# A Fourier-mixing layer and an ELU MLP on one core: DRAM reads of Z and Bs by writing unit, w_out in 4 KB runs, the bias spread by a matmul

## The chip, the core and the metric

The kernel runs on one core of a Trainium2 chip. A core has five engines with queues of their own: TensorE (PE, with its weight loads shown as PEld), VectorE (DVE), ScalarE (ACT), GpSimd (POOL) and SyncE (SP, which here only issues transfers). The metric is the device time of one launch in microseconds; less is better.

## The reference

The input x has 8 sequences of 3008 positions and 256 channels, in float32. Each sequence goes through a real Fourier transform over its positions, a complex 256x256 linear map with a bias, a soft threshold at 0.01, and the inverse transform. Each position's 256 numbers then go through a two-layer network with 2048 hidden units and an ELU between.

```python
X = np.fft.rfft(x, axis=1)                       # x: (8, 3008, 256)
Yr = Xr @ w_r - Xi @ w_i + b_r
Yi = Xr @ w_i + Xi @ w_r + b_i
Yr = np.sign(Yr) * np.maximum(np.abs(Yr) - 0.01, 0.0)      # Yi likewise
y = np.fft.irfft(Yr + 1j * Yi, n=3008, axis=1)
h = y @ w_in                                     # w_in: (256, 2048)
g = np.where(h > 0, h, np.exp(np.minimum(h, 0)) - 1)
out = g @ w_out                                  # w_out: (2048, 256)
```

## The kernel before

**Transform in four matmul stages.** 3008 is 47 x 64, so the transform of a sequence is made of one over 64 points (stage A), one over 47 points (stage X), the linear map with the threshold (stage M), and back over 64 points (stage B) and 47 points (stage Y). The twiddle tables M1 to M4 are computed on the chip in the prologue: iota on POOL, range reduction on DVE, sine on ACT. Stages A, M, B and Y sum over a different index than the one that the stage before left on the partitions, and twice that takes a trip through DRAM: A's results go to a DRAM tile DA (L155, L157) and come back as Z, with 96 partitions of 32 slots (`load_Z`, L159 to L164); B's results go to DB (L260, L265) and come back as Bs, four tiles of 96 partitions and 8 slots (`load_Bs`, L267 to L272).

A sequence is 6 A units, 8 X units, 12 M groups, 6 B units and 8 Y units. X unit u reads slots 8(u//2) to 8(u//2)+8 of Z, on all 96 partitions, and Y unit u reads the one tile Bs of its slots. One A unit writes four of the 24 rows of DA, one B unit four of the 24 rows of DB; the row index lies on the partitions of what is read back, so every slot of Z needs all six A units.

**The network.** `front` (L705) makes 256 hidden units of 512 positions as four matmuls (L715), ACT takes the exponential, DVE and POOL finish the ELU (L740, L742, L752, L754), and `back` (L757) multiplies with w_out (L773), two slots later. A slot is one such half block. 47 slots make one sequence.

**Order of the work.** It is written out by hand, engine by engine, in program order. The prologue does stages A to B of sequence 0 and A of sequence 1, with dummy matmuls (`idle_pe`, L295) in PE's gaps. Then the main loop (L844) runs 376 slots; `plan` (L800) puts one unit of the next sequence's transform into most slots (`f0`, before `front`), and loads and other small work after it (`f1`). The four Bs loads of a sequence are put behind A unit 1, the two Z loads behind A unit 5.

**Queues.** SP issues the DA, Z, DB, Bs, w_in, bias and output transfers in program order and waits in place: a load that waits for a write's landing holds everything behind it. POOL issues x (L116) and w_out (L583) among its arithmetic; `gate` (L585) is a tiny POOL copy that makes POOL wait for a tile before it issues what follows.

**Bias.** `bias_bc` holds the bias on all 128 partitions; it is read from DRAM with a zero step over 128 partitions (L526 to L530) and added by DVE (L202). For half of the first sequence's M groups PE adds it instead: `bias_p` holds the bias as three bfloat16 summands in partitions 0, 32 and 64, and a matmul with ones spreads it (L189). Six small loads (L304) and DVE and ACT steps (L601, L602, L607 to L610) make `bias_p`.

**Weights of the network.** w_out comes in two transfers in runs of 1 KB, w_in in four quarters that are scaled to bfloat16 by `scale_w_in` (L655): quarters 0 and 1 on DVE, 2 on ACT, 3 on DVE in two halves in slots 3 and 4. Four POOL instructions (L520 to L523) cast w_r and w_i into `wcat_r` and `wcat_s`.

Of the kernel before, what the change touches and what calls it, by code (L numbers as in the profile page):

```python
# [8 lines left out]
ALU = mybir.AluOpType  # L9
# [10 lines left out]
N1 = 47  # L20
# [9 lines left out]
def kernel(  # L30
# [47 lines left out]
    zp = ctx.enter_context(tc.tile_pool(name="zp", bufs=1))  # L78
    wk2 = ctx.enter_context(tc.tile_pool(name="wk2", bufs=2))
    wk3 = ctx.enter_context(tc.tile_pool(name="wk3", bufs=3))  # L80
    wk4 = ctx.enter_context(tc.tile_pool(name="wk4", bufs=4))
# [47 lines left out]
    def unit_A(b, u, alone=False, on_dve=False, ahead=False):  # L129
        ci, uu = u // 2, u % 2  # L130
        if uu == 0:
            if ahead and ci > 0:
                A_of[b, ci] = late3.tile([P, 8, D], BF16, name="A", tag="gT")
            elif alone:
                A_of[b, ci] = wk4.tile([P, 8, D], BF16, name="A", tag="Bs")
            else:
                A_of[b, ci] = wk2.tile([P, 8, D], BF16, name="A", tag="A")
# [3 lines left out]
        dav = DA_of[b].rearrange("j p d -> p j d")  # L141
# [9 lines left out]
        )  # L151
        j0 = 8 * ci
# [6 lines left out]
    def load_Z(b, s0, s1):  # L159
# [3 lines left out]
        dv = DA_of[b].rearrange("j (h c s) d -> (j h c) s d", h=2, c=2)  # L163
        nc.sync.dma_start(Z_of[b][:, s0:s1, :], dv[:, s0:s1, :])  # L164
# [102 lines left out]
    def load_Bs(b, w):  # L267

        Bs = wk4.tile([4 * K1, 8, D], BF16, name="Bs", tag="Bs")
        dv = DB_of[b].rearrange("k (c h m) d -> (k c h) m d", c=2, h=2)  # L270
        nc.sync.dma_start(Bs[:], dv[:, 8 * w : 8 * w + 8, :])
        Bs_of[b, w] = Bs  # L272

    def unit_Y(b, u, alone=False, on_dve=False):
# [3 lines left out]
        yT, Bs = yT_of[b], Bs_of[b, w]  # L278
        ps = unit_ps("yps", alone)
        psv = ps[:].rearrange("p a (k j) -> p (a k) j", j=P)  # L280
        for j in range(8):
            nc.tensor.matmul(  # L282
                psv[:, j, 0 : 2 * N1], lhsT=Bs[:, j, dt * P : dt * P + P], rhs=M4[:],
# [16 lines left out]
    brow, rest = (wk3.tile([P, 2 * D], F32, name="yb", tag="yb") for _ in range(2))  # L300
    nc.vector.memset(brow[:], 0.0)
    for o, bv in ((0, b_r), (D, b_i)):
        for k in range(3):
            nc.sync.dma_start(  # L304
                brow[32 * k : 32 * k + 1, o : o + D],
                bass.AP(tensor=bv.tensor, offset=bv.offset, ap=[[0, 1], [1, D]]),
            )
    idle_pe(9)
    xts = []
# [3 lines left out]
    with tc.tile_pool(name="stagep", bufs=1) as stagep:  # L313
# [41 lines left out]
        pcol = iota("pcol", [P, 1], [[0, 1]], cm=1)  # L355
        srow = iota("srow", [P, 2 * NS], [[0, 2], [1, NS]])
# [52 lines left out]

        k4h = col(dve, qcol, 0.5, ALU.mult, -0.25, ALU.add)  # L410
# [87 lines left out]
        pool.tensor_tensor(v4[:], v4[:], r4[:], ALU.subtract)  # L498

# [17 lines left out]
        fA(5)  # L517
        nc.sync.dma_start(w_r_f[:], w_r.rearrange("(c p) e -> p c e", p=P))
        nc.sync.dma_start(w_i_f[:], w_i.rearrange("(c p) e -> p c e", p=P))
        pool.tensor_copy(wcat_r[:, :, 0:D], w_r_f[:])  # L520
        pool.tensor_copy(wcat_r[:, :, D : 2 * D], w_i_f[:])
        pool.tensor_scalar(wcat_s[:, :, 0:D], w_i_f[:], -1.0, None, ALU.mult)
        pool.tensor_copy(wcat_s[:, :, D : 2 * D], w_r_f[:])  # L523
        for g in range(4):
            load_Z(0, 8 * g, 8 * g + 8)
        for o, bv in ((0, b_r), (D, b_i)):  # L526
            nc.sync.dma_start(
                bias_bc[:, o : o + D],
                bass.AP(tensor=bv.tensor, offset=bv.offset, ap=[[0, P], [1, D]]),
            )  # L530
# [31 lines left out]
        idle_pe(40)  # L562
# [6 lines left out]
    w_out_v = moe_w_out.rearrange("(t p) e -> p t e", p=P).bitcast(F32R)  # L569
# [3 lines left out]
    def load_w_in(q):  # L573
        if q < 3:
# [6 lines left out]
    def load_w_out(hh):  # L581
        hf = slice(hh * NFT // 2, (hh + 1) * NFT // 2)
        nc.gpsimd.dma_start(w_out_r[:, hf, :], w_out_v[:, hf, :])  # L583

    def gate(src):  # L585

        t = gatep.tile([P, 1], F32, name="gate", tag="gate")
        nc.gpsimd.tensor_copy(t[0 : src.shape[0], :], src)
# [6 lines left out]
    gate(Z_of[0][:, 8, 0:1])  # L595
    for ci in range(3):
        load_x(1, ci)
# [301 lines left out]
```

## Time and profile before

| What | us |
|---|---|
| median of three runs (lowest, highest) | 912.54 (911.84, 913.92) |
| the profiled execution: its own time | 911.36 |
| the profiled execution: span of its records | 909.6 |
| PE busy in the span | 893.2 (98%) |
| first X matmul of sequence 0 | 23.25 |
| first M matmul with all of XT there | 30.50 |
| first Y matmul of sequence 0 | 55.16 |
| PE busy between 66 and 880 | 810.55 of 814 |

The time is that of a whole launch; the span runs from the first to the last record of the core. Up to 66 us the kernel is in its prologue and in the filling of the main loop's pipeline; from there PE runs almost without a gap to the end. In the views below a line names the source line, engine, operation and tile; what stands in brackets is the idle time of the engine ahead of it and what ended it.

### The profile page before, as it was taken

The numbers are of one execution on the slowest core, as the hardware profiler recorded it, in microseconds if no ns is written. First come the engines' busy times: TensorE is split into PE (matmuls) and PEld (weight loads), VectorE is DVE, ScalarE is ACT, GpSimd is POOL, SyncE is SP. The second block draws the span as 40 slices with busy tenths as digits, with TensorE's granted clock in tenths as the row PEclk, the third lists the DMA queues.
The fourth block names the chain that finished last, engine by engine and source line by source line (L and its number), as shares of the span: only waits on it lengthen the run. The fifth ranks groups of instructions, "written<-read, shape, count | busy, mean of one in ns | idle before, by whom it ended". The sixth has DMA issues, their size and how long they took to land.

```text
span 909.6 us, 17270 instructions
## 1 busy us (share of the span) xinstructions
PE 893.2 (98%) x6721; PEld 652.3 (72%) x6721; DVE 717.5 (79%) x891; ACT 696.8 (77%) x850; POOL 314.9 (35%) x438
## 2 busy tenths in 40 slices
PE   8989999999999999999999999999999999999997
PEld 3447667876688667886678766787667866777775
DVE  8669778887788778897788877888778877778776
ACT  6768788777878778787787888778887877767664
POOL 6701540333321441405404153033332134443664
PEclk9999999999999999999999999999999999999999
DMA  8997116721283215732166032752228111231011
GB/s 270 309 269 228 47 48 186 209 70 47 77 241 124 71 47 143 190 109 85 56 201 194 24 99 59 217 161 72 69 72 230 30 42 47 82 82 48 24 48 46
DMA packets 90670, 106.24 MB, mean 117 GB/s; under 512 B 5270, under 2 KB 81308, under 8 KB 87228
## 3 DMA queue, kind: packets, MB, share of 16 engines
q1 hardware_dynamic: 84332, 77.62, 30.6%
q0 software_dynamic: 5968, 27.26, 9.1%
q8 instruction: 52, 0.85, 0.4%
q10 hardware_dynamic: 288, 0.26, 0.1%
q14 instruction: 30, 0.25, 0.1%
HBM read 55.32 MB, written 49.81 MB: 116 GB/s over the span
## 4 chain that ended last, share of the span: by engine, by line
PE 85%; DVE 5%; ACT 3%; DMA 3%; issue 2%; POOL 1%; SPq 1%; DVEq 0%; ACTq 0%; POOLq 0%
PE ps_o L773 34%; PE hps L715 34%; PE mps L192 9%; PE yps L282 2%; PE bps L244 2%; PE xps L175 2%; PE aps L144 2%; DMA Bs<-DB 2%; DVE gT L742 1%; DVE Et L754 1%; ACT Et L729 1%; ACT Et L726 1%; DMA xt<-in_x_dram 1%; DVE osb L784 1%; ACT Bz L257 1%
## 5 line engine op out<-in xcount | busy, mean ns | idle before, releaser
L773 PE MATMUL ps_o<-w_out_r,gT 128*128 128x256 f32 x3008 | 477.0, 301 | 0.2 <-DVE gT L740 0.2
L773 PEld LDWEIGHTS ps_o<-w_out_r,gT 128*128 128x128 f32 x3008 | 403.4, 189 | 50.3 <-DVE osb L784 1.3
L715 PE MATMUL hps<-yT,w_in_s 128*128 128x512 bf16 (+4 forms) x1728 | 389.9, 353 | 2.5 <-DVE gT L742 1.2
L740 DVE SCALAR_TENSOR_TENSOR gT<-Et,hps 128x512 fp32r<-128x512 f32 (+1 forms) x272 | 222.8, 848 | 75.3 <-POOL Et L752 38.2
L742 DVE SCALAR_TENSOR_TENSOR gT<-hps,Et 128x1024 fp32r<-128x1024 f32 x198 | 242.2, 1223 | 16.5 <-PE ps_o L773 1.0
L715 PEld LDWEIGHTS <-w_in_s 128*128 128x128 bf16 x1728 | 141.6, 98 | 129.4 <-issue 23.0
L729 ACT ACTIVATE Et<-hps 128x1024 f32<-128x1024 f32 x198 | 204.0, 1030 | 13.2 <-PE hps L715 6.7
L752 POOL TENSOR_SCALAR Et<-Et 128x512 f32<-128x512 f32 x187 | 111.4, 615 | 222.9 <-ACT Et L724 222.9
L754 DVE TENSOR_SCALAR Et<-Et 128x1024 f32<-128x1024 f32 x198 | 137.0, 692 | 48.0 <-ACT Et L729 40.1
L210 POOL TENSOR_SCALAR clip<-yb 128x512 f32<-128x512 f32 x84 | 51.7, 615 | 316.0 <-DVE yb L202 278.6
L724 ACT ACTIVATE Et<-hps 128x512 f32<-128x512 f32 x188 | 102.1, 595 | 63.9 <-PE hps L715 63.9
L726 ACT ACTIVATE Et<-hps 128x1024 f32<-128x1024 f32 x84 | 86.3, 1027 | 71.5 <-PE hps L715 71.0
L211 POOL TENSOR_TENSOR Y<-yb,clip 128x512 bf16<-128x512 f32 x84 | 107.2, 1276 | 7.0
L727 ACT ACTIVATE Et<-Et 128x1024 f32<-128x1024 f32 x84 | 88.8, 1058 | 2.7
L202 DVE TENSOR_TENSOR yb<-mps,bias_bc 128x512 f32<-128x512 f32 x89 | 61.4, 689 | 35.4 <-PE mps L192 28.6
L127 ACT CAST XT<-xps 128x768 bf16<-128x768 f32 x61 | 48.8, 800 | 15.8 <-PE xps L175 15.8
L127 ACT CAST yT<-yps 128x752 bf16<-128x752 f32 x63 | 49.7, 788 | 14.2 <-PE yps L282 14.1
L192 PE MATMUL mps<-wcat_r,XT 128*128 128x512 bf16 x192 | 58.2, 384 | 0.8 <-ACT Bz L257 0.3
L127 ACT CAST A<-aps 128x1024 bf16<-128x1024 f32 x45 | 45.6, 1014 | 15.3 <-PE aps L144 13.8
L192 PE MATMUL mps<-wcat_s,XT 128*128 128x512 bf16 x192 | 57.1, 379 | 0.0
L192 PEld LDWEIGHTS <-XT 128*128 128x128 bf16 x384 | 30.8, 98 | 29.6 <-DVE XT L125 0.6
L257 ACT CAST Bz<-bps 128x1024 bf16<-128x1024 f32 x46 | 46.0, 1000 | 2.5 <-PE bps L244 2.5
(110 smaller groups left out, 412.9 us busy)
## 6 DMA issues: line engine op xcount, KB each, us to landing
xt<-in_x_dram POOLq DMA_DIRECT2D x21, 1024.0 KB, 7.1
out_dram<-osb SPq DMA_DIRECT2D x158, 128.0 KB
Bs<-DB SPq DMA_DIRECT2D x32, 384.0 KB
DA<-A SPq DMA_DIRECT2D x21, 512.0 KB
DB<-Bz SPq DMA_DIRECT2D x21, 512.0 KB
Z<-DA SPq DMA_DIRECT2D x7, 1152.0 KB
Z<-DA SPq DMA_DIRECT2D x11, 384.0 KB
xt<-in_x_dram POOLq DMA_DIRECT2D x6, 512.0 KB, 5.9
```

Source lines behind the costliest of these rows:

```text
L127: nc.scalar.copy(dst, src)
L192: nc.tensor.matmul(ps, lhsT=XT[:, dt, c, o : o + P], rhs=wm[:, dt, :], start=(not biased and m == 0 and dt == 0), stop=(m == 1 and dt == 1),)
L211: nc.gpsimd.tensor_tensor(Y_of[b, q][:, i, :], yb, clip[:], ALU.subtract)
L715: nc.tensor.matmul(hps[:, s, c0:c1], lhsT=w_in_s[:, dt, ft * P : ft * P + P], rhs=yT_of[b][:, dt, t0 : t0 + c1 - c0], start=(dt == 0), sto ...
L724: nc.scalar.activation(E_[:, s], hps[:, s], AF.Exp)
L726: nc.scalar.activation(E_, hps[:], AF.Relu, scale=-1.0)
L729: nc.scalar.activation(E_, hps[:], AF.Exp)
L740: nc.vector.scalar_tensor_tensor(o, e, -1.0, h, ALU.add, ALU.max)
L742: nc.vector.scalar_tensor_tensor(o, h, 0.0, e, ALU.max, ALU.add)
L752: eng.tensor_scalar(E_[:, s], E_[:, s], 1.0, 0.0, ALU.min, ALU.max)
L754: nc.vector.tensor_scalar(E_, E_, 1.0, -1.0, ALU.min, ALU.add)
L773: nc.tensor.matmul(po[q][:, i_ % 2, :], lhsT=gT[:, s, i_ * P : i_ * P + P], rhs=w_out_r[:, ft, :], start=(ft == 0 and i_ % 2 == 0), stop=( ...
```

## The change

Four edits, and an order of the prologue that goes with them.

1. **Z and Bs are read by writing unit.** `load_Z(b, u)` reads the four rows of DA that A unit u wrote into partitions u, u+6, ... u+90 of Z, 16 runs of 16 KB; `load_Bs(b, v)` does the same with B unit v and one Bs tile of 32 slots. So there are six loads each per sequence, and each waits for the write of its own unit. Z's rows now lie in another order over the partitions, which seven tiny DVE instructions bring into the column values that the tables M2 and M4 are computed from (`sixth` to `c0`). In the main loop the loads stand one slot behind the write that they need, Bs not ahead of the slot after Y unit 7 of the sequence before.
2. **w_out in four transfers with 4 KB runs.** A partition holds four neighbouring rows of w_out; w_in's columns are reordered to match, in the scaling (`scale_w_in` reads with a step of four numbers). Quarters 2 and 3 of w_in are scaled by DVE in halves in slots 1 to 4.
3. **The bias.** Two small loads put it on 128 partitions (`b4`), five tiny POOL steps split it into three bfloat16 summands (`bp3`), a DRAM tile `bd` turns them into three rows of `bias_p`, and one matmul with ones and a DVE copy make `bias_bc`.
4. **Order.** w_r and w_i are issued behind Z; their casts go from POOL to DVE, between the X units; the first subtraction for M3 goes from DVE to POOL; `Abs` for M3 (L606) goes behind the X units; the load of the Exp table (L627) goes from the M stage to behind B unit 5; 35 dummy matmuls instead of 40 ahead of the X units.

```diff
-    def load_Z(b, s0, s1):
+    def load_Z(b, u):
...
-        dv = DA_of[b].rearrange("j (h c s) d -> (j h c) s d", h=2, c=2)
-        nc.sync.dma_start(Z_of[b][:, s0:s1, :], dv[:, s0:s1, :])
+        dv = DA_of[b][4 * u : 4 * u + 4].rearrange("j (r s) d -> (j r) s d", r=4)
+        nc.sync.dma_start(Z_of[b][u : 2 * NR : 6], dv)
...
-    def load_Bs(b, w):
-        Bs = wk4.tile([4 * K1, 8, D], BF16, name="Bs", tag="Bs")
-        dv = DB_of[b].rearrange("k (c h m) d -> (k c h) m d", c=2, h=2)
-        nc.sync.dma_start(Bs[:], dv[:, 8 * w : 8 * w + 8, :])
-        Bs_of[b, w] = Bs
+    def load_Bs(b, v):
+        if b not in Bs_of:
+            Bs_of[b] = bsp.tile([P, NS, D], BF16, name="Bs", tag="Bs")
+        dv = DB_of[b][4 * v : 4 * v + 4].rearrange("k (r m) d -> (k r) m d", r=4)
+        nc.sync.dma_start(Bs_of[b][v : 4 * K1 : 6], dv)
...
-    brow, rest = (wk3.tile([P, 2 * D], F32, name="yb", tag="yb") for _ in range(2))
-    nc.vector.memset(brow[:], 0.0)
...
+    for o, bv in ((0, b_r), (P // 2, b_i)):
+        nc.sync.dma_start(b4[o : o + P // 2, :], bv.rearrange("(p j) -> p j", j=4))
+    bd = dram.tile([P, 3, 4], BF16, name="bd", tag="bd")
+    nc.vector.memset(bias_p[:], 0.0)
...
+        sixth = col(dve, pcol, 1.0 / 6.0, ALU.mult, -5.0 / 12.0, ALU.add)
+        rcol = col(dve, sixth, CMAGIC, ALU.add, -CMAGIC, ALU.add)
+        zcol = mix(dve, rcol, -95.0, p16, ALU.mult, ALU.add)
+        half = col(dve, zcol, 0.5, ALU.mult, -0.25, ALU.add)
+        qcol = col(dve, half, CMAGIC, ALU.add, -CMAGIC, ALU.add)
+        c1 = mix(dve, qcol, -2.0, zcol, ALU.mult, ALU.add)
+        c0 = col(dve, c1, -1.0, ALU.mult, 1.0, ALU.add)
...
+        for k in range(3):
+            pool.tensor_copy(bp3[:, k, :], b4[:])
+            if k < 2:
+                pool.tensor_tensor(b4[:], b4[:], bp3[:, k, :], ALU.subtract)
...
         fA(5)
+        nc.sync.dma_start(bd[:], bp3[:])
+        for u in range(6):
+            load_Z(0, u)
+            if u == 3:
+                nc.sync.dma_start(
+                    bias_p[0:3, :].rearrange("k (p j) -> k p j", j=4),
+                    bd.rearrange("p k j -> k p j"),
+                )
         nc.sync.dma_start(w_r_f[:], w_r.rearrange("(c p) e -> p c e", p=P))
         nc.sync.dma_start(w_i_f[:], w_i.rearrange("(c p) e -> p c e", p=P))
-        pool.tensor_copy(wcat_r[:, :, 0:D], w_r_f[:])
...
-        for g in range(4):
-            load_Z(0, 8 * g, 8 * g + 8)
-        for o, bv in ((0, b_r), (D, b_i)):
-            nc.sync.dma_start(
-                bias_bc[:, o : o + D],
-                bass.AP(tensor=bv.tensor, offset=bv.offset, ap=[[0, P], [1, D]]),
-            )
...
-        idle_pe(40)
+        nc.scalar.activation(r4[:], v4[:], AF.Sin, bias=0.0, scale=TURN)
+        pool.tensor_scalar(w3[:], v3[:], CMAGIC, -CMAGIC, ALU.add, ALU.add)
+        pool.tensor_tensor(w3[:], v3[:], w3[:], ALU.subtract)
+        idle_pe(35)
+        bps_ = pre1.tile([P, 2 * D], F32, name="mps1", tag="mps1")
+        nc.tensor.matmul(bps_[:], lhsT=busy[:, 0:P], rhs=bias_p[:], start=True, stop=True)
+        nc.vector.tensor_copy(bias_bc[:], bps_[:])
...
+        for u in range(8):
+            unit_X(0, u, alone=True, on_dve=u in (1, 4, 7))
+            if u in (1, 4):
+                for dst, src, sc in casts[u // 2 : u // 2 + 2]:
+                    dve.tensor_scalar(dst, src[:], sc, None, ALU.mult)
+            if u == 0:
+                t = stagep.tile([P, 1], F32, name="gate")
+                pool.tensor_copy(t[:], w_i_f[:, 1, D - 1 : D])
+                for ci in range(3):
+                    load_x(1, ci)
+            idle_pe(1)
...
-    w_out_v = moe_w_out.rearrange("(t p) e -> p t e", p=P).bitcast(F32R)
+    NQ = NFT // 4
+    w_out_v = moe_w_out.rearrange("(q p t) e -> q p t e", p=P, t=NQ).bitcast(F32R)
...
     fB(2)
+    load_Bs(0, 0)
+    load_w_out(1)
...
     fB(3)
-    load_w_in(2)
+    load_Bs(0, 1)
     first_M(5, 1, True)
     let_go()
     fB(4)
+    load_Bs(0, 2)
+    load_Bs(0, 3)
     idle_pe(3)
     fB(5, True)
+    load_Bs(0, 4)
+    load_Bs(0, 5)
+    nc.scalar.activation(dume[:], busy[:, 0:1], AF.Exp, scale=0.0)
...
+        dst = dst.rearrange("p c (t m) -> p c t m", t=NQ)
+        src = src.rearrange("p c (m t) -> p c t m", t=NQ)
...
+    gate(Bs_of[0], 64, 4 * K1, 0)
+    load_w_out(2)
+    load_w_out(3)
     for u in range(6):
         unit_A(1, u, on_dve=bool(u % 2), ahead=True)
+        if u % 2:
+            write_A(1, u)
+            if u < 5:
+                load_w_in(2 + u // 2)
...
-            if u == ("A", 1):
-                f1[t] += [(load_Bs, (n1, w)) for w in range(4)]
-            if u == ("A", 5) and n2 < B:
-                f1[t] += [(load_Z, (n2, s0, s1)) for s0, s1 in ((0, 8), (8, NS))]
+            if u[0] == "B" and u[1] % 2:
+                at_ = max(t, seq.index(("y", 7)) + lead) + 1
+                f1[at_] += [(load_Bs, (n1, u[1] - 1)), (load_Bs, (n1, u[1]))]
+            if u[0] == "A" and u[1] % 2 and n2 < B:
+                f1[t + (u[1] < 5)] += [(load_Z, (n2, u[1] - 1)), (load_Z, (n2, u[1]))]
         if b == 0:
-            f1[3].append((scale_w_in, (3, True, 0)))
-            f1[4].append((scale_w_in, (3, True, 1)))
+            for t in range(4):
+                f1[t + 1].append((scale_w_in, (2 + t // 2, True, t % 2)))
```

## The prediction

> **What bounds the kernel now.** I read the page's totals first, then the waits of PE after 66 us, the prologue as a list of instructions, the chain that ended last, the busy table by stretches, and the DMA queues.
>
> ```profile
> span 909.6 us, 17270 instructions
> PE 893.2 (98%) x6721; PEld 652.3 (72%) x6721; DVE 717.5 (79%) x891; ACT 696.8 (77%) x850; POOL 314.9 (35%) x438
> ```
>
> PE is the bound. Only 16.4 us of the span are not PE, so the change can win little, and only where PE waits or runs dummy matmuls. PE's waits from 66 us on, and then the two places of the largest kind:
>
> ```profile
> PE yps L282 <- DMA Bs<-DB: 1.9, 2, 1.0
> PE yps L282 <- ACT Bz L257: 0.4, 2, 0.2
> ...
> 149.35 0.51 PE L282 MATMUL yps<-M,Bs 96*128 96x94 bf16 x8 [0.91 <-DMA Bs<-DB]
> ...
> 797.83 0.51 PE L282 MATMUL yps<-M,Bs 96*128 96x94 bf16 x8 [1.03 <-DMA Bs<-DB]
> ```
>
> So 843 us of the run hold 1.9 us for Bs; the rest of the gain must come from the first 66 us. There, PE waits for Z:
>
> ```profile
> 18.40 1.74 SPq L164 DMA_DIRECT2D Z<-DA  x4
> 23.25 0.51 PE L175 MATMUL xps<-M,Z 96*128 96x96 bf16 x8 [0.43 <-DMA Z<-DA]
> 24.74 0.51 PE L175 MATMUL xps<-M,Z 96*128 96x96 bf16 x8 [0.19 <-DMA Z<-DA]
> 30.50 0.39 PE L192 MATMUL mps<-wcat_r,XT 128*128 128x512 bf16 x1 [0.33 <-DVE XT L125]
> ```
>
> Later, in the chain of waits, for the last DB write and then the first Bs load:
>
> ```profile
> 48.19 2.77 DMA DB<-A
> 51.15 3.97 DMA Bs<-DB
> 55.16 0.85 PE yps L282 x16
> ```
>
> And the granted clock (second number from behind, ahead of the DMA share) halves after that gap:
>
> ```profile
> 54.00:55.00 1.00, 0.15 (x1) 0.00 (x0) 0.32 (x1) 0.00 (x0) 0.00 (x0) 1.00 0.95 283
> 58.00:59.00 1.00, 1.00 (x11) 0.72 (x10) 0.00 (x0) 0.87 (x1) 0.00 (x0) 0.50 1.02 254
> 59.00:60.00 1.00, 1.00 (x4) 0.38 (x3) 0.71 (x2) 0.83 (x2) 0.63 (x2) 0.50 0.97 229
> ```
>
> Two slots later DVE, in the list of instructions, waits with its operands ready:
>
> ```profile
> 63.25 1.23 DVE L742 SCALAR_TENSOR_TENSOR gT<-hps,Et 128x1024 fp32r<-128x1024 f32 x1 [1.04 <-PE ps_o L773]
> 64.53 1.02 PE L715 MATMUL hps<-yT,w_in_s 128*128 128x512 bf16 x4 [0.96 <-DVE gT L742]
> ```
>
> **The change, part by part** (gains negative).
>
> *Tables.* One more iota on POOL (0.14, as pcol) goes ahead of the first x transfer. Seven DVE steps of 0.15 to 0.17 delay the table chain by 1.1; DVE's idle 0.73 at 12.7 and 0.23 at 16.7 take most, so the last sine ends near 21.5 instead of 21.2. Z comes later than that: nothing. If Z came by 21.5, the tables would be late next.
>
> *Start of X.* Before, all four Z loads wait until the last DA write has landed (18.40), behind w_r, w_i (0.52 MB) in the same queue. After, loads 0 to 3 need writes that landed earlier and follow the last DA write from about 16 on; loads 4 and 5 wait as before, SP standing still meanwhile, with w_r, w_i and w_in behind them. DA's 256 KB of unit 5 and its neighbours fill the DMA engines until 18.35 (busy 0.94 from 14 to 18), so what counts is bytes: 1.57 MB of Z, of which some 0.24 MB can take the place that w_r's bytes had, leaves 1.33 MB. At 300 GB/s (what Z alone ran at around 22 to 24) that ends at 22.8; at 256 GB/s (18 to 23) at 23.5, at 350 at 22.2. SP issues at 0.43 each, six Z, bd and the bias row, 3.4 in all, within that. I take 22.8, the middle rate being Z's own: **-0.45** (-1.0 to +0.25). The 35 dummies of 0.22 from 14.0 end at 21.7, so PE idles a little longer than before; one bias matmul (0.22) and a DVE copy of 512 (0.69 as L202) fit there. Two 128 KB bias reads go away behind Z.
>
> *Pace of X.* Before, 7.2 from the first X matmul to the last copy's end (30.45), since PE waited for each later group of Z. With all of Z there, unit u+2 waits only for unit u's PSUM copy: matmuls 0.51, ACT 0.80, DVE 0.95. Followed through the eight units, that is 6.4. The four casts are now DVE's, 0.42 each (the 128x512 scaling row), two behind unit 1 and two behind unit 4; both fit, if w_i has landed by about 25 (22.8 plus 0.52 MB at 256 GB/s gives 24.9). If not, DVE holds unit 4. **-0.8** (-1.0 to -0.2). POOL loses 5.8 of casts, gains 2.8 to 3.5 for w3 (its 0.61 and 1.27 rows times 1.5), then the gate and the x issues, about as early as now (26.2).
>
> *M3.* ACT's Abs (0.85) leaves unit 1 for the place behind unit 6, and both sines and DVE's first M3 product come some 0.95 later against the M stage. Ahead of the first B unit (35.13) POOL's Y ended at 34.75, so 0.4 is covered: **+0.4** (0 to +0.85). The 1.28 table load leaves the M stage, where PE never waited for it. POOL issues two w_out pieces among its Y work; two such halves took 1.12 and 0.97, here there are four smaller ones; B unit 3 has a whole pair (2.5) of cover for that.
>
> *Start of Y.* Four of the six Bs loads now move during B. The last two wait for the last DB write, 2.77 as before, then 2.2 to 3.0 for 2 x 256 KB on queues with less in them (the 256 KB write took 2.77): ready 53.2 to 54.0 on the old scale, not 55.1. Then the A units are next: the Exp load with its dummy (1.48) now stands ahead of A unit 0's copy, which ends at 49.96 instead of 48.52, and the PSUM pairs pass on 0.3 or so, until PE, with five dummies at its end, comes to Y at 54.2 to 54.9. Gain 0.5. PE no longer idles a microsecond before Y, so the first slots run at full clock: three matmuls took 1.07 instead of 0.65. Together **-0.9** (-1.5 to -0.3).
>
> The clock row is 0.50 although PE had been busy for most of 50 to 54. The Trainium skill, "TensorE: Matmul & The Clock Gate", section "Part 1: The HAM clock gate", names a window of about 3.4 us with too little activity as the condition; by it the shorter gap after the change keeps full clock, and the sum is the one above. If the gate closed anyway, 0.42 would come back.
>
> *Filling of the pipeline.* gT of slot 1 stands 1.04 although Et and hps were there; its buffer is the one that A unit 3's write still reads, issued at 55.70 behind 768 KB of Bs and a w_in quarter. PE loses 1.0 at 64.53. The write now comes some 2.5 earlier with less ahead, though two w_out pieces start beside it. Against that, DVE scales four halves (0.42 each) in slots 1 to 4 instead of two, and its slot (0.69 + 1.23 + 0.42 = 2.34) is over PE's 2.15: 0.2 for each new one. **-0.7** (-1.06 to +0.7). Upper end: a read with a step of four numbers might cost DVE one number per cycle, as STT rows do: 0.69 a half, 1.23 instead of 0.68 a quarter. I take 0.42, the same operation and shape.
>
> *Main loop.* At 143.24 and 793.41 four loads were issued together, and the first took 4.4 to land; now two remain at that place, the other four a few slots earlier. Half the bytes: 1.5 sooner, less up to 0.5 since Y needs the last load. Both waits go: **-1.7** (-1.9 to 0). SP issues six transfers more per sequence (2.3 at 0.38), and waits some 3.5 (789.86 to 793.35) at each pair behind its write. Behind it stand output writes, whose buffer is wanted two blocks (34 us) later, and DB and DA writes, four slots on. Nobody waits.
>
> **Sum:** -0.45 - 0.8 + 0.4 - 0.9 - 0.7 - 1.7 = -4.15, with ends -6.5 and +1. The profiled execution took 911.36, 1.8 over its span and 1.2 under the median, 912.54. From the median: **908.4**.
>
> **Rivals.**
>
> *A. The bias row holds up Z.* Reading bd as three rows is 384 runs of 8 bytes, in the queue between Z loads 3 and 4. In the first 14 us this queue had
>
> ```profile
> q1 hardware_dynamic: 1312, 0.66, 15.8%
> ```
>
> that is 0.158 x 16 x 14 / 1312 = 27 ns a packet of 512 bytes. Over 16 engines the runs are 24 x 27 = 0.65, no matter. Over three engines they are 128 x 27 = 3.5, with Z's last 16 KB runs behind them on these engines, and the bias matmul stands in PE's queue ahead of X: X starts near 26.3, and the sum loses 3.5: **911.9**. For it: three is the outer size of that transfer; against it: SP waits there anyway, and 8 bytes may cost less than 27 ns. The Trainium skill, "DMA: Bandwidth & Descriptors", section "Why a DMA increments its semaphore by 16 and not by 1", says that the engine count is the largest one up to 16 that divides both sides' slowest dimension, so three here; by it this rival's place is right and only the price per run is open. No row here shows it.
>
> *B. DVE binds the filling.* At 0.69 a half and 1.23 a quarter the A units' copies come 0.5 later and slots 1 to 4 lose 0.5 each instead of 0.2: **910.0**. Nothing in the trace has that step.
>
> *C. The loads of one tile go one after another* (the other side). Six loads write interleaved partitions of one tile. If each is held until the one before has landed (2.8, as the DB write), Z takes 6 x 2.8 from 16: X starts at 33 instead of 22.8, the last Bs 2.8 later: **about 921**. It decides from 1.5 a load on. Against it:
>
> ```profile
> 1.96 0.93 SPq L304 DMA_DIRECT2D yb<-in_b_r_dram  x3
> ```
>
> Three loads into partitions 0, 32 and 64 of one tile go out in 0.93, with no wait between.
>
> *D. SP's waits reach an engine* in the main loop: one late DB write costs what is seen now, 1.0; once in each of seven sequences gives **915**. PE's waits above show none but the two.
>
> **How the numbers follow.** My forecast 0.60, A 0.13, B 0.12, C 0.08, D 0.07. A measurement here tells 0.2% (1.8 us) from no change. Forecast: faster 0.57, same 0.03; B: 0.09 and 0.03; A: 0.02, 0.10 and 0.01 slower; C and D slower. So faster 0.68, same 0.16, slower 0.16. Range: A with some reserve above, 913.0, leaves out C and D, 0.15; the forecast's best ends together, below 905.8, 0.06.
>
> **What the profile after will show.** X's first matmul near 22.8 (26 for A, 33 for C) and 6.4 to the M stage; the first B unit some 0.4 behind an M matmul, waiting for DVE or POOL; Y about 24.5 behind the M stage's start, with no clock below 0.9 after it; gT of slot 1 without a wait for anything but Et; no wait of PE for Bs after 66. Wrong would be: Z after 24, a long DVE wait for w_i among the X units, DVE scaling rows over 0.5 a half, or new waits of PE behind SP in the main loop.

## The result, and the profile after

| | before | after |
|---|---|---|
| median, us (lowest, highest) | 912.65 (911.84, 913.92) | 925.77 (925.1, 928.55) |
| ratio, 95% interval | | 1.0148 (1.0124 to 1.0172) |
| the profiled execution: its own time, span | 911.36, 909.6 | 925.35, 923.3 |

The change made the kernel 13 us slower; 908.4 was forecast, and the range ended at 913.0. The totals of the page of after:

```profile
span 923.3 us, 17326 instructions
PE 902.1 (98%) x6717; PEld 659.0 (71%) x6717; DVE 716.3 (78%) x898; ACT 695.6 (75%) x848; POOL 315.3 (34%) x444
```

PE is busy 8.9 us more, with no matmul more: its instructions became longer. The other 4.8 us are PE's waits. The 13.7 us of span, cut at events that both traces have (the forecast's terms are put beside the stretch that they speak of):

| stretch of the first sequence | before | after | difference | forecast |
|---|---|---|---|---|
| start to the first X matmul | 23.25 | 28.41 | +5.16 | -0.45 |
| X: first matmul to last copy | 7.19 | 8.47 | +1.28 | -0.8 |
| to the first B matmul | 4.69 | 4.96 | +0.27 | +0.4 |
| B matmuls | 11.69 | 12.06 | +0.37 | 0 |
| to the first Y matmul | 8.34 | 9.91 | +1.57 | -0.9 |
| to the first w_out matmul | 6.77 | 8.14 | +1.37 | -0.7, with the next row |
| to the sixth slot's w_out matmuls | 11.87 | 11.79 | -0.08 | |
| the rest, 370 slots | 835.78 | 839.56 | +3.78 | -1.7 |

So 10 of the 13.7 us lie ahead of the main loop and 3.8 in it. PE's waits from 20 to 66 us (total, times, longest):

```profile
PE mps L582 <- DMA bias_p<-bd: 4.3, 1, 4.3
PE yps L289 <- DMA Bs<-DB: 2.0, 1, 2.0
PE xps L182 <- DMA Z<-DA: 1.8, 1, 1.8
PE hps L744 <- DVE yT L125: 1.0, 1, 1.0
```

SP's issues ahead of X in after (start, duration, what):

```profile
16.51 2.57 SPq L171 DMA_DIRECT2D Z<-DA  x4
19.18 0.45 SPq L540 DMA_DIRECT2D bias_p<-bd  x1
19.68 4.65 SPq L171 DMA_DIRECT2D Z<-DA  x2
```

and what PE had of it:

```profile
26.02 0.58 PE L582 MATMUL mps<-bias_p,busy 128*128 128x512 bf16 x1 [4.28 <-DMA bias_p<-bd]
28.41 0.80 PE L182 MATMUL xps<-M,Z 96*128 96x96 bf16 x8 [1.80 <-DMA Z<-DA]
```

The first four loads are issued early, as the change says. Then SP, which issues the transfers in program order, stands 4.0 us on the issue of Z load 4, right behind the bias row, and PE stands first for the bias row and then for Z. An X unit takes 0.80 where it took 0.51, and the busy table says why (the granted clock is the third number from behind; 0.50 is half of full speed):

```profile
24.00:28.00 4.00, 0.58 (x1) 0.00 (x0) 0.69 (x1) 0.00 (x0) 2.25 (x2) 0.51 0.81 201
28.00:32.00 4.00, 3.59 (x33) 2.80 (x34) 1.64 (x3) 1.42 (x2) 2.22 (x4) 0.50 0.44 100
65.00:69.00 4.00, 3.32 (x15) 1.64 (x16) 0.96 (x2) 1.53 (x3) 0.29 (x1) 0.50 1.08 352
```

The clock is half from 24.1 to 34.3, through most of X, and again from 65.0 to 71.9, through the filling of the pipeline. The chain of waits between B and the main loop in after:

```profile
56.91 3.30 DMA DB<-A
60.22 3.35 DMA Bs<-DB
63.81 0.51 PE yps L289 x8
64.34 10.24 DMA DA<-A
74.70 1.22 DVE gT L771
```

The last DB write leaves at 56.91, though its data were there at 55.24 (the end of unit 5's copy), and the last DA write takes 10 us until the third gT (the third slot's input to the w_out matmuls, which takes over the buffer that this write reads) can be made. In the main loop the list of PE's waits has no row for Bs, but this one stands for a Y unit, at the second place where before waited:

```profile
810.73 0.49 PE L289 MATMUL yps<-M,Bs 96*128 96x94 bf16 x8 [0.84 <-issue]
```

### The profile page after: what moved, and what is told of

It reads as the page before. It is cut to its first block, busy times and chain, and to the rows that moved or that the text cites. A ratio compares the mean times of both kernels' runs of the same rounds, so it can differ in the third digit from the quotient of the medians.

```text
span 923.3 us, 17326 instructions
## 1 busy us (share of the span) xinstructions
PE 902.1 (98%) x6717; PEld 659.0 (71%) x6717; DVE 716.3 (78%) x898; ACT 695.6 (75%) x848; POOL 315.3 (34%) x444
## 4 chain that ended last, share of the span: by engine, by line
PE 87%; DMA 4%; DVE 3%; ACT 3%; POOL 1%; issue 1%; SPq 0%; DVEq 0%; ACTq 0%; POOLq 0%
PE ps_o L802 36%; PE hps L744 34%; PE mps L199 8%; PE xps L182 3%; PE yps L289 2%; PE bps L251 2%; PE aps L145 2%; DMA DA<-A 1%; ACT Bz L264 1%; DMA Bs<-DB 1%; DMA xt<-in_x_dram 1%; POOL Y L238 1%; ACT Et L755 1%; DVE gT L771 1%; DMA Z<-DA 0%
## 5 line engine op out<-in xcount | busy, mean ns | idle before, releaser
L802 PE MATMUL ps_o<-w_out_r,gT 128*128 128x256 f32 x3008 | 483.2, 303 | 0.1
L802 PEld LDWEIGHTS ps_o<-w_out_r,gT 128*128 128x128 f32 x3008 | 407.7, 189 | 50.1 <-DVE osb L813 1.1
L127 ACT CAST XT<-xps 128x768 bf16<-128x768 f32 x61 | 48.6, 799 | 24.1 <-PE xps L182 24.1
```

Source lines behind the costliest of these rows:

```text
L127: nc.scalar.copy(dst, src)
L802: nc.tensor.matmul(po[q][:, i_ % 2, :], lhsT=gT[:, s, i_ * P : i_ * P + P], rhs=w_out_r[:, ft, :], start=(ft == 0 and i_ % 2 == 0), stop=( ...
```

## The experiments

What is said of a run's stretches is worked out from its trace, as in the table above; times are medians, and ratios, with a 95% interval in brackets, are to runs of before made beside them (912.2 to 913.2). One trace is one execution, and stretches ahead of the main loop differ between executions by about 1 us with nothing changed in them: X takes 7.1 to 8.4 us in the versions of before whose X is untouched, and starts at 27.98 to 29.11 in the five versions whose start of X is that of after (after, pad_after, bs_last, da_first, loads_early). What follows is to be read against that.

### The main loop: where tiles lie in SBUF

The w_out matmuls, grouped by line and shape (total us, mean ns), in before and in after:

```profile
L773 PE MATMUL ps_o<-w_out_r,gT 128*128 128x256 f32 x3008 | 477.0, 301 | 0.2 <-DVE gT L740 0.2
```

```profile
L802 PE MATMUL ps_o<-w_out_r,gT 128*128 128x256 f32 x3008 | 483.2, 303 | 0.1
```

6.2 us more for the same 3008 matmuls; from start to start, taken over neighbours less than 0.2 us apart, they step by 116.2 and 118.4 ns. The change did not touch them. It did add two small tiles, `b4` and `bp3`, 64 bytes per partition together, behind w_out_r in the constant pool, so that every later tile moved by 64 bytes: by the tiles' sizes w_out_r stays at 64 modulo 128, and gT goes from 0 to 64. Two runs put 64 unused bytes at that place, in before and (so that it makes 128) in after:

```diff
+    pad = constp.tile([P, 16], F32, name="pad")
+    nc.vector.memset(pad[:], 0.0)
     xts = []
```

pad_before:

> The kernel before with one unused tile of 64 bytes per partition ahead of the x tiles, so that everything allocated behind it (x, Z, yT, Et, gT) lies 64 bytes further on, as it does after the change. Theory 1 (the place in SBUF costs the 2 ns that each w_out matmul lost): w_out matmuls at 303 ns mean as after, not 301; each sequence of 47 slots 0.6 to 0.9 longer; 917 to 918.5. Theory 2 (the lost 2 ns come from the new order of w_out and w_in, or from the chip): 912.6, no difference.

pad_after:

> The kernel after with another unused 64 bytes, 128 in all. Theory 1 (place in SBUF): the w_out matmuls are back at 301 ns, the sequences at 108 instead of 108.6, 920 to 921. Theory 2: 925.8 as after.

pad_before took 917.07, ratio 1.0051 (1.0041 to 1.006), with 118.4 ns a step; pad_after 923.41, 1.0119 (1.0102 to 1.0136), with 116.7. In pad_after the same group reads

```profile
L804 PE MATMUL ps_o<-w_out_r,gT 128*128 128x256 f32 x3008 | 478.6, 301 | 0.2 <-DVE gT L771 0.2
```

Is it gT's own place or its distance from what did not move, w_out_r above all? place_all has the 64 bytes at the head of the pool, so that everything moves:

```diff
     constp = ctx.enter_context(tc.tile_pool(name="constp", bufs=1))
+    pad = constp.tile([P, 16], F32, name="pad")
     M1 = constp.tile([P, P], F32R, name="M1")
```

> The kernel before, with 64 unused bytes per partition at the head of the constant pool, so that every tile moves by 64 bytes and their distances stay. (The first placement run put the 64 bytes behind w_out_r, so that only the later tiles moved.) Theory 1, the absolute place of gT decides: as in that run the w_out matmul steps by 118.4 ns instead of 116.2, the main loop is 4 to 5 us longer, about 917.3. Rival, the distance of gT from w_out_r decides (it stays 64 modulo 128): 116.2 ns a step, 912.5 to 913.5, no change.

912.82, 1.0002 (0.9993 to 1.0011), 116.2 ns: moving all tiles by 64 bytes does nothing, the theory of the absolute place fell, a distance counts. Two more runs put 32 and 96 bytes (`[P, 8]` and `[P, 24]`) at the place of pad_before, for distances of 96 and 32 modulo 128:

> The kernel before with 32 unused bytes per partition behind w_out_r, so that the distance from w_out_r to gT goes from 64 to 96 modulo 128. Theory 1, only equal places modulo 128 (distance 0) cost: 116.2 ns a step, 912.5 to 913.5. Rival, 64 is the one good distance: 117.3 to 118.4 ns a step, 915 to 917.5. Second rival, these are faster still: below 115 ns, below 909.

> As pad32 with 96 bytes: distance 32 modulo 128. The same three readings: 912.5 to 913.5 (only 0 costs), 915 to 917.5 (only 64 is good), below 909 (32 and 96 are better). If it differs from pad32, the side of the shift counts too.

917.51, 1.0048 (1.0032 to 1.0064), 118.5 ns, and 917.32, 1.0051 (1.0036 to 1.0066), 119.1 ns. So the kernel before stands at the one good distance of the four tried, and any of these small tiles behind w_out_r costs it some 4.5 us. Other tiles moved with gT, so the pair is an inference from the group that lengthened; the two-layer network's first matmul kept its mean (381 and 382 ns). The group lengthens by more than the kernel does (3008 times 2.2 ns are 6.6 us, the time 3.9 to 4.7). In the changed kernel the place is worth 2.4 us by pad_after. That run's main loop still takes 1.1 us longer than before's, and its w_out matmuls still step by 116.7 ns instead of 116.2, 1.6 us in the group's sum; what of, stays open.

### The main loop: the waits for Bs

bs_main is before with one part of the change: Bs by unit from the second sequence on (six loads as in the change's diff, M4's columns to match). The first sequence reads the same partitions by slot groups, as before:

```diff
+    def load_Bs0(w):
+        dv = DB_of[0].rearrange("(v k) (r m) d -> (k r) v m d", v=6, r=4)
+        nc.sync.dma_start(Bs_of[0][0 : 4 * K1, 8 * w : 8 * w + 8, :], dv[:, :, 8 * w : 8 * w + 8, :])
```

> The kernel before, with one part of the change alone: from the second sequence on Bs is read by six loads of one unit's output each, two units behind the write, into every sixth partition; the first sequence reads the same partitions by slot groups as before, at the same places, and everything else is as before, places in SBUF modulo 128 included. Theory 1, this part does what was predicted and its gain was covered by the place of the tiles: both waits for Bs at 149 and 798 go, no new wait of PE comes, 910.8 to 911.7 (ratio 0.9985). Rival, the standing of SP behind its pairs reaches an engine, or the loads of 16 KB runs slow the engines' reads: 912.5 to 916.

913.48, ratio 1.0012 (1.0003 to 1.0021). Neither wait went:

```profile
151.01 0.49 PE L291 MATMUL yps<-M,Bs 96*128 96x94 bf16 x8 [0.47 <-DMA Bs<-DB]
...
799.45 0.49 PE L291 MATMUL yps<-M,Bs 96*128 96x94 bf16 x8 [0.90 <-DMA Bs<-DB]
```

Slot by slot, the two slots are 0.46 and 0.13 shorter than in before (0.79 and 0.17 in after). From the issue of the last DB write to the Y matmul at the second place it is 789.86 to 797.83 in before, 7.97, and 791.58 to 799.45 here, 7.87; in place_all, before_da and before_wlate, which load Bs as before does, it is 7.67, 8.17 and 7.91. So half the bytes in the last loads won nothing there that is clear of the spread, and 0.2 to 0.4 at the first place (10.35 from write to Y; 10.54 to 10.79 in the four versions that load Bs as before): there are two loads of 16 KB runs, Y needs the second, its issue ends 1.2 after that of the first began, and it takes 3.2 more. From the sixth slot on the kernel takes what before takes (835.79 and 835.78), so the 1 us by which the whole is slower lies ahead of it. X took 8.1 us, which is within the spread; whether this version's ten small table steps have a part was not tried.

### The start of X: the bias row, the order, the rate

bias_late takes the bias row out of the way:

```diff
-            if u == 3:
-                nc.sync.dma_start(bias_p[0:3, :]..., bd...)
         nc.sync.dma_start(w_i_f[:], ...)
+        nc.sync.dma_start(bias_p[0:3, :]..., bd...)
...
-        nc.tensor.matmul(bps_[:], lhsT=busy[:, 0:P], rhs=bias_p[:], ...)   # to behind the X units
```

> The kernel after with the bias row's 384 runs of 8 bytes issued behind Z, w_r and w_i, and the bias matmul with its copy behind the X units. Theory 1 (these runs keep SP from issuing Z loads 4 and 5: their first packets went out at 24.49, after load 3's had ended near 23.6): issue of load 4 takes 0.6 instead of 4.0, loads 4 and 5 follow load 3 without a gap, X starts near 26.5 instead of 28.4, 923.9. Theory 2 (16 KB runs by themselves are slow to issue and to land, the bias row does not matter): X at 28 as after, 925.5.

926.88, ratio 1.0154 (1.0139 to 1.0169). SP's issues now run through:

```profile
16.30 3.74 SPq L171 DMA_DIRECT2D Z<-DA  x6
```

so the 4.0 us were the bias row's. But X starts only 0.7 earlier, at 27.72: the wait for the bias stood in front of a wait for Z. After's packets say the same: from 23.70 to 24.49, 0.8 us, no byte of Z moves. z_slots goes further: on top of bias_late it reads Z of every sequence by groups of slots again, as before, with w_r and w_i still behind it in the first:

```diff
-        for u in range(6):
-            load_Z(0, u)
+        for g in range(4):
+            load_Z(0, 8 * g, 8 * g + 8)      # the load_Z of before; M2's columns as before
```

> As bias_late, and Z read by groups of 8 slots as before the change, four loads behind the last DA write, ahead of w_r and w_i (M2's columns in the old order again). Theory 1 (X is late because no unit can start before all six loads are there): first group by 20.5 to 21.5, X from 21.5, the M stage from 28.5 instead of 36.9, the TensorE clock at full rate throughout; 917 to 918. Theory 2 (what follows, x of the next sequence and the casts, is bound by its own transfers): X as in theory 1, but the first slot of the main loop gains less than 4; 921 or more.

924.92, 1.0134 (1.0113 to 1.0154). X starts at 22.68, but its last copy ends at 32.88 and B starts at 40.25, since DVE waits 3.0 and 1.7 for w_r and w_i in the middle of X. z_w, otherwise as z_slots, has them ahead of Z, as before:

```diff
+        nc.sync.dma_start(w_r_f[:], w_r.rearrange("(c p) e -> p c e", p=P))
+        nc.sync.dma_start(w_i_f[:], w_i.rearrange("(c p) e -> p c e", p=P))
         for g in range(4):
             load_Z(0, 8 * g, 8 * g + 8)
```

> The changed kernel with the reading of Z undone: four loads by groups of slots, behind w_r and w_i as before, and the bias row and its matmul behind X; Bs, w_out, w_in and the casts on DVE stay as changed. Theory 1, the start of X is the largest share of the loss: X starts at 22.6 to 23.5, its last copy ends at 30.5 to 32 (w_r and w_i are there for the casts, which z_slots lacked), everything behind moves up by 5 to 6, and the time is 919.5 to 921.5. Rival, the DMA engines set the start of the main loop and give the gain back there: the sixth slot stays at 82.5 to 84, 924 to 926.

922.86, 1.0112 (1.0099 to 1.0126): X starts at 24.75, later than hoped, Y at 59.37 and the sixth slot at 80.62, 4.4 and 3.1 earlier than in after. The time lies between the two theories: of 3.7 us won at X, 2.9 arrive. What holds X in after was told apart by z_halves, which takes bias_late, keeps the changed partitions and halves each load:

```diff
-        for u in range(6):
-            load_Z(0, u)
+        for s0 in (0, 16):
+            for u in range(6):
+                load_Z(0, u, s0, s0 + 16)
```

> bias_late (bias row and its matmul out of the way) with each Z load split in two halves of slots: first the six first halves, then the six second halves, 8 KB runs, same partitions and bytes. Theory 1, X waits because all six loads of 16 KB runs must be complete: X starts after half of the bytes, 23 to 24.5 instead of 27.7, though X's copies may then wait for w_r and w_i (X's end 34 to 35 instead of 35.9); time 925 to 926.5. Rival, the last DA write's landing and SP's issue times (12 x 0.45) set it: X starts at 26 or later.

922.27, 1.0113 (1.0091 to 1.0136). X starts at 24.52, 3.2 earlier than in bias_late, although the bytes come no faster, and the time is 4.6 less. By the packets' records:

| Z of sequence 0 | first packet | a quarter there | half there | all there | X starts |
|---|---|---|---|---|---|
| before, four loads by slots | 19.4 | 21.3 | 22.7 | 26.8 | 23.25 |
| after, six loads by unit | 18.0 | 21.1 | 22.5 | 27.1 | 28.41 |
| bias_late, six loads by unit | 17.7 | 21.2 | 23.1 | 26.5 | 27.72 |
| z_halves, twelve loads | 19.1 | 21.6 | 23.3 | 28.0 | 24.52 |

From the first packet to the last Z comes at 172 to 212 GB/s in all four. Before starts X with the first quarter and lets the rest come beside X; by unit, X needs the last byte.

### The clock

keep_warm has 64 dummy matmuls ahead of X instead of 35, 12 ahead of Y instead of 3, and 3 behind Y:

```diff
-        idle_pe(35)
+        idle_pe(64)
...
-    idle_pe(3)
+    idle_pe(12)
     for u in range(2):
         unit_Y(0, u, alone=True, on_dve=bool(u % 2))
+    idle_pe(3)
```

> The changed kernel with 64 dummy matmuls ahead of X instead of 35, 12 ahead of Y instead of 3, and 3 more behind Y's first two units: PE is busy until Z and Bs are there. Theory 1, the half clock lengthens X and the filling: granted clock 1.0 through X, X from its first matmul to its last copy 7.0 to 7.3 instead of 8.5, from Y's first matmul to the first w_out matmul 7.0 to 7.4 instead of 8.1; the time is 923.3 to 924.3. Rival, copies and loads set the pace there and PE has slack at half clock: both stretches stay within 0.3 of what they were, 925.5 to 926.

```profile
28.00:32.00 4.00, 2.60 (x30) 1.44 (x29) 1.68 (x3) 0.96 (x2) 0.90 (x3) 1.00 0.43 129
```

The clock stays full. X takes 6.37 instead of 8.47, Y to the first w_out matmul 6.74 instead of 8.14: both as the theory has it, and slightly more. The time is 928.04 all the same, ratio 1.0171 (1.0154 to 1.0187). X starts 1.5 later (29.92, with Z's last byte at 28.64), the first to the sixth slot take 14.75 instead of 11.79, and Y waits 1.97 for Bs at 161.8. What the clock gave at the first w_out matmul was gone at the sixth slot.

### Start of the main loop: SP's order and the DMA engines

bs_last puts the two loads that DB's last write stood behind after it:

```diff
     fB(4)
-    load_Bs(0, 2)
-    load_Bs(0, 3)
     idle_pe(3)
     fB(5, True)
+    load_Bs(0, 2)
+    load_Bs(0, 3)
```

> The changed kernel, with the loads of Bs pieces 2 and 3 issued behind B unit 5 and its DB write instead of ahead of them. Theory 1, DB's last write stood in SP's queue behind a load that waited for an earlier write: the write now goes at about 55.3 instead of 56.9, and Y starts 1.5 to 2.3 us earlier, at 61.5 to 62.3 instead of 63.8; the time is 923.5 to 924.3 (ratio to before about 1.012). Rival, the bytes of Bs and w_in and w_out on the DMA engines decide, in whatever order: Y starts at 63.5 or later, 925.5 to 926.

Y starts at 62.57, 1.2 earlier (1.05 counted from the end of the B matmuls), and the first w_out matmul at 69.31, 2.6 earlier; the time is 925.4, 1.0139 (1.0123 to 1.0154), as without. Again the sixth slot comes late (84.70; 83.74 in after), and the list of DVE's instructions has the reason, the wait of the third gT:

```profile
74.66 1.22 DVE L771 SCALAR_TENSOR_TENSOR gT<-hps,Et 128x1024 fp32r<-128x1024 f32 x1 [2.50 <-DMA DA<-A]
```

In after it comes at 74.70. da_first, on top of bs_last, puts w_in's quarters 2 and 3 behind the DA writes:

```diff
             write_A(1, u)
-            if u < 5:
-                load_w_in(2 + u // 2)
...
+    load_w_in(2)
+    load_w_in(3)
     for u in range(6):
         load_Z(1, u)
```

> The kernel of bs_last (the changed one with Bs pieces 2 and 3 behind the last DB write), and w_in quarters 2 and 3 loaded behind the second sequence's three DA writes instead of between them. There the first w_out matmul came 2.6 us earlier than in the changed kernel, and the sixth slot 1.0 later. Theory 1, the DMA queues: the third DA write reads the buffer that the third gT wants, and its bytes stood behind w_in and w_out, so that gT waited until 74.66 in both; with w_in behind it the third gT comes by 72.5, the sixth slot's w_out by 81.5 to 82.5 instead of 84.7, and the time is 922 to 923.3. Rival, all of these bytes are needed by the sixth slot and it comes at 84 or later in whatever order (w_in waits instead of DA): 925 to 926.

928.57, 1.0177 (1.0163 to 1.0191): the theory fell as it was put. The DA write is no longer late, but now DVE waits ahead of the second gT, for the weights:

```profile
72.90 0.61 DVE L686 TENSOR_SCALAR w_in_s<-w_in_f 128x512 bf16<-128x512 f32 x1 [3.76 <-DMA w_in_f<-in_moe_w_in_dram]
```

loads_early, on top of bs_last too, brings the weights forward instead, w_out's first piece ahead of M and w_in's quarters behind B units 0 to 2:

```diff
     load_w_in(0)
+    load_w_out(0)
...
     fB(0)
+    load_w_in(1)
...
     fB(1)
-    load_w_in(1)
+    load_w_out(1)
+    load_w_in(2)
...
     fB(2)
     load_Bs(0, 0)
-    load_w_out(1)
+    load_w_in(3)
...
             write_A(1, u)
-            if u < 5:
-                load_w_in(2 + u // 2)
```

> The kernel of bs_last, with the loads of the weights moved forward: w_out's first piece ahead of the M stage instead of behind its fifth group, its second behind B unit 1, and w_in's quarters 1, 2 and 3 behind B units 0, 1 and 2 (there quarter 1 went behind unit 1, and 2 and 3 among the second sequence's A units). Theory 1, bytes that the change put behind the B units hold the third gT until 74.7: with 1 to 1.5 MB less there (3 to 5 us at 314 GB/s) it comes at 70 to 72, the sixth slot at 81.5 to 82.5 instead of 84.7, and the time is 922 to 923.5. Rival, Bs and DA alone keep it late, or the earlier loads delay the DB writes: 925 or more.

926.22, 1.0146 (1.013 to 1.0162): it fell too. gT no longer waits for DMA, but Bs comes later (PE waits 2.8 ahead of Y, which starts at 64.29), and the third gT is at 74.46 once more. Three orders, those of after, bs_last and loads_early, and one time (76.64 in da_first). From the end of the B matmuls to the third gT, the busy table has in before

```profile
46.82:65.11 18.29, 15.13 (x90) 8.01 (x91) 10.95 (x12) 10.58 (x12) 1.47 (x2) 0.91 0.95 271
```

and in after

```profile
53.90:74.70 20.80, 16.72 (x95) 8.70 (x96) 12.61 (x14) 11.20 (x14) 1.30 (x3) 0.84 1.01 314
```

(the last two numbers are the DMA share and GB/s): the DMA engines are full, and move 18.29 x 271 = 5.0 MB before and 20.80 x 314 = 6.5 MB after. Of the 1.5 MB more, 1.0 is POOL's queue, 0.27 MB in the first stretch and 1.26 in the second, most of it w_out's second half: before issues that half at 59.87, behind all three DA writes, and after issues it at 64.17, beside the last one (64.34). before_wlate puts more bytes into the stretch of the kernel before, with one edit:

```diff
         load_x(1, ci)
-    load_w_out(0)
...
     fB(4)
+    load_w_out(0)
```

> The kernel before, with one edit: w_out's first half (1 MB) is loaded behind B unit 4 instead of ahead of X. Nothing waits for it there by itself (its first reader comes at 62). Theory 1, the DMA engines bind from the end of B to the third gT: that gT comes 2 to 3.3 later than 65.1 (1.05 MB at 271 to 330 GB/s), less up to 1 that Z, w_in and x win by the free engines in front; time 914 to 916. Rival, there is room and the bytes fit: 912 to 913.3.

915.36, 1.0032 (1.002 to 1.0044): 1 MB, which nobody waits for itself, moved behind B costs 3.1 us. The third gT comes 3.9 later, at 69.02, PE waits 3.8 for Bs ahead of Y, and the busy table has

```profile
46.94:69.02 22.08, 16.14 (x90) 8.47 (x91) 11.15 (x13) 10.57 (x12) 1.07 (x2) 0.85 1.01 285
```

Not all of the 3.9 is waiting for bytes: behind the longer gap the clock is half from 58.3 to 65.2 instead of 57.5 to 60.9, and Y to the first w_out matmul takes 7.76 instead of 6.77. Not tried was the edit that the bytes suggest for the kernel after, w_out's second half behind the last DA write.

### Together

mended takes the edits of z_w, bs_last, da_first and pad_after, and five more dummies ahead of Y. mended2 takes those of z_w, bs_last, loads_early and pad_after, and three more dummies:

> z_w, the order of da_first, the 64 bytes of pad_after, and five more dummy matmuls ahead of Y: of the change stay the six Bs loads by unit, w_out in 4 KB pieces with the strided scaling, the bias by a matmul and the casts on DVE. If the four causes found are all there is (Z's reading 5 to 6, the order of SP's loads 2.5, places in SBUF 2.4, the clock about 1): 912 to 914.5. If the remaining parts cost on their own (scaling at 0.61 a half, tables, casts): 915 to 918.

> The kernel of mended (Z by groups of slots behind w_r and w_i, the 64 bytes, Bs pieces 2 and 3 behind the last DB write, more dummies ahead of Y) with the weights loaded as in loads_early. mended came to its first w_out matmul at 65.5 and to its sixth slot only at 82.3, DVE waiting 2.8 for w_in. Theory 1: from the first to the sixth slot 11.8 to 12.8 instead of 16.8, sixth slot at 77.5 to 79, time 916 to 918. Rival, the strided scaling or the DMA engines still hold it: 919 or more.

921.15, 1.0088 (1.0073 to 1.0102), and 918.97, 1.0072 (1.0051 to 1.0093). The first misses both of its theories. mended loses 16.8 us between first and sixth slot, DVE waiting 2.8 for w_in as in da_first; mended2 takes 12.0 there, as its first theory has it, and 1 us more in all. Of its 6.7 us of span over before, 2.1 lie between B and Y (PE waits 1.9 for Bs), 1.6 ahead of X, 1.6 behind the sixth slot, 1.2 in X, M and B. before_da tried to better the kernel before by that order:

```diff
             load_w_out(1)
-            load_w_in(3)
...
+    load_w_in(3)
     for s0, s1 in ((0, 8), (8, NS)):
         load_Z(1, s0, s1)
-    idle_pe(3)
+    idle_pe(6)
```

> The kernel before, with its last w_in quarter loaded behind the second sequence's DA writes instead of between them, and three more dummy matmuls ahead of Y. If the wait of 1.0 for gT's buffer at 64.5 is the DA write standing behind these 512 KB, and the half clock of 57.5 to 60.9 comes of the gap ahead of Y: 911.0 to 911.8. Rival, w_in then comes too late for its own scaling, or the copies of Y set the pace: 912.3 to 914.

914.01, 1.0031 (1.0008 to 1.0053): gT still waits 0.72 for the DA write, and nothing is won. Four of its twelve executions took 919 to 922 us, the others 912.0 to 914.6; the profiled one, 912.65, is of the others, so what held the four is not shown. No version beats the kernel before.

## Why the prediction was wrong

**Tables (0).** Right: the last sine of X's tables ends at 21.25, as in before (21.20), well ahead of Z.

**Start of X (-0.45 forecast, +5.16).** The step that failed is the rate with its count of bytes: 1.33 MB at 300 GB/s, from 18.35 to 22.8. Z's first byte moved at 18.0, so none of it took the place of w_r's bytes, and it ran at 172 GB/s from its first packet to its last (1.57 MB from 18.0 to 27.1), below the lower end that was priced, 256; without the bias row in between it was 179 (bias_late). X starts 1.3 behind the last byte. And the comparison was wrong in kind: before's 23.25 is the time of a quarter of Z. The same trace had its last byte, at 26.8; that row bounds a start that needs all of Z. Rival A had the right place, SP and PE did stand for the bias row, and the wrong price: by bias_late it is worth 0.7 at X and nothing in the time, the rest is Z itself. Rival C (loads one after another) did not occur: four go out in 2.6 us. That its 921 is the figure nearest to the measured time is chance.

**Pace of X (-0.8, +1.28).** The working gave 6.4; with the clock full it is 6.37 (keep_warm). What failed is the sentence that PE idles "a little longer" ahead of X: its last dummy ended at 21.7, and with one matmul at 26.0 it stood until 28.4, and X ran at half clock. The mechanism was right, its condition not: here the granted clock fell to half at 24.1, 2.3 us after the last dummy, and keep_warm, without the idling, had full clock through X and Y. The Trainium skill, "TensorE: Matmul & The Clock Gate", "Part 1: The HAM clock gate", has the clock fall after a window of about 3.4 us, which runs freely, with too little activity. The trace agrees with the window: in after the clock changes at 24.07, 34.31, 65.03 and 71.86, and these times lie 3, 9 and 2 times 3.41 us apart. The window that ended at 24.07 was not all idle: dummies ran in it until 21.7.

**M3 (+0.4).** +0.27 to the first B matmul, which waits 0.2 for POOL's Y, as said; another 0.37 in B.

**Start of Y (-0.9, +1.57).** The step that failed: four Bs loads "now move during B". Two of them did. Pieces 2 and 3 were issued ahead of DB's last write and waited for earlier writes, so that SP held that write from 55.24 to 56.91; bs_last gets 1.2 of it back at Y. The gap ahead of Y grew to 2.0 instead of shrinking, and the clock halved behind it, for 1.4 (8.14 against 6.74 in keep_warm). The reading that a shorter gap keeps full clock does not hold by the length of the gap alone: before's clock halved behind a wait of 1.0 for Bs, and it stayed full behind 1.1 in pad_before, 1.3 in pad32 and 1.9 in mended2.

**Filling (-0.7, +1.29 over the two rows).** Slot 1's gT no longer waits for a DA write, as the working had it. What failed is that nothing was to take that wait's place: it passed to the third gT, whose buffer the last DA write reads. That write leaves SP at 64.34, behind two quarters of w_in and beside w_out's second half, and takes 10.24. In after itself it ends only 0.45 behind DVE's other work; there the +1.37 ahead of the first w_out matmul is the half clock named above, and the five slots behind it take what they took before (11.79 and 11.87). In keep_warm and bs_last, which come to the first w_out matmul 2.0 and 2.6 earlier, the wait grows to 1.87 and 2.50 and the sixth slot is no earlier. So what no term held is the traffic of this stretch. The trace of before showed the DMA engines busy there (0.95 to 1.02 from 54 to 60 in the lines quoted in the prediction); it was read for the clock and not for the DMA share. Shown by before_wlate is that 1 MB more in this stretch of before costs 3.1 us; that bytes explain each order of the changed kernel is inferred, and in loads_early the third gT does not wait for DMA. The scaling with a step of four numbers takes 0.61 a half and 1.08 a quarter, where 0.42 and 0.68 were taken; rival B's 0.69 and 1.23 were nearer.

**Main loop (-1.7, +3.78).** Two steps. "1.5 sooner" failed: in bs_main both waits remain, in after the second (0.84; in pad_after both, 0.41 and 0.91); 0.1 of 7.97 is won from write to Y at the second place, which is within the spread, and 0.6 (bs_main) to 1.0 (after) in the two slots, of which up to 0.4 is within it too. And a cost that no term held, since it has no line in the diff of the main loop: two tiles of 64 bytes together that moved gT against w_out_r, 2.4 us in after and 3.9 to 4.7 in before. Another 1.1 of the main loop, by pad_after, stays open. That SP's standing reaches no other engine (against rival D) was right: from 72 us on PE's waits in after are that one of Y and none other over 0.2.

**The sum.** The upper ends of the terms add up to +1.3, not +1, and 912.5 less 6.5 is 906.0, not 905.8. In the busy rows the granted clock is the third number from behind, not the second; its values were read rightly. None of this changes the outcome.

## What to carry to other kernels

Ask of a producer's read-back not when its bytes begin but which byte the first consumer needs: an order that lets every load start earlier can still make the consumer wait for the last one. Before moving a "hidden" transfer, read the DMA share of the stretch that it moves to; at 0.95 one megabyte more cost 3.1 us here (before_wlate). And a new small tile in front of large ones is an edit of their places: compare the mean duration of matmuls that were not touched.

## What the hardware showed that was not expected

- The w_out matmul, 128x256 fp32r, stepped by 116.2 ns when w_out_r and gT lay 64 bytes apart modulo 128, and by 118.4 to 119.1 at 0, 32 and 96 (3008 matmuls; 4.5 us of 912). That this pair is the cause is inferred, since other tiles moved with gT.
- A load of 384 runs of 8 bytes moved in 0.8 us (9 ns a packet), but with four loads of Z ahead of it the next issue in the same queue stood for 4.0 us; behind Z, where nothing follows it, it cost nothing that was seen.
- A DVE scaling of 128x512 took 0.42 us with neighbouring numbers and 0.61 when it read with a step of four.
- The length of a gap did not decide alone whether PE's clock halved: it did behind a wait of 1.0 us (before, half from 57.5 to 60.9) and did not behind 1.9 (mended2).
